# Attention, MoE and FFN in one kernel: V's two heads laid on alternating partitions, both loads on SP's queue

## The chip, the core and the metric

The kernel runs on one core of a Trainium2 chip. The core has a matrix engine (TensorE, PE in the profile, with its weight loads as PEld), three engines for elementwise work (VectorE as DVE, ScalarE as ACT, GpSimd as POOL), a sequencer that only issues (SyncE, SP) and 16 DMA engines that all queues share. The metric is the device time of one execution in microseconds (us); less is better.

## The reference

Three steps follow one another: attention over chunks of 32 queries with a context of 56 keys plus 8 memory keys, a mixture of 8 experts with one expert per token, and a dense FFN. The attention is what the change touches.

```python
# q, k, v: (4, 8, 768, 64) f32; mem_k, mem_v: (4, 8, 8, 64)
for c in range(S // 32):
    l_start, r_end = max(0, 32 * c - 16), min(S, 32 * c + 32 + 8)
    k_full = concat([mem_k, k[:, :, l_start:r_end]], axis=2)
    v_full = concat([mem_v, v[:, :, l_start:r_end]], axis=2)
    scores = (q_c @ k_full.T) / 8
    a = exp(scores - max(scores)); a = a / (sum(a) + 1e-9)
    out_c = a @ v_full
...
x = moe(out.reshape(3072, 512))      # top-1 of 8 experts, w1: 512x1024, w2: 1024x512
return (relu(x @ w_in) ** 2) @ w_out # 512x2048, 2048x512
```

## The kernel before, in words

The host lays q and k out as (batch, pair of heads, 128, 768), two heads of 64 dimensions on 128 partitions, and cuts v into windows: for each batch and head 64 rows (56 context keys and 8 memory keys) of 24 chunks by 64 dimensions, 6 KB per row.

`attention` runs over 32 steps `i`: 4 batches, 4 pairs of heads, 2 halves of 384 queries. One step works on both heads of a pair for 12 chunks. The loop is software-pipelined; in iteration `i` the list `order` calls, in this sequence:

- `stage_b(i)` on PE: scores of 12 chunks (24 matmul passes) into the PSUM tile `sp`. The moving operand is `kw`, the key windows of a pair: head 0 on partitions 0 to 63, head 1 on 64 to 127, each head with columns of its own and zeros in the other's, so that one matmul makes the scores of both heads. `sp` is (query, tile, head, key).
- `stage_d(i-2)` on PE: P times V into `op`, 12 chunks. V's tile `vb` is block-shaped too: head 0's 64 key rows on partitions 0 to 63 in the columns of head 0, head 1's on 64 to 127 in those of head 1, zeros elsewhere.
- `stage_m`, `sum_b(i-1)`, `inv_b(i-1)`, `max_b(i)`, `sub_b(i)`: the logits of the router on PE; row sums, reciprocals, row maxima and the subtraction on DVE.
- `stage_c(i-1)` on PE: the transpose of `e` into `tp`, which ACT copies to `pt`, the stationary operand of `stage_d`. Its partitions are (head, key), the order of `vb`'s rows.
- `exp_b(i)` on ACT, `scale_d(i-2)` on DVE (into `xa`), `stage_t`, `stage_u`.

After the list, `windows(i+2)` lets POOL copy the key windows into `kw` (three buffers), one copy per head and one for the memory keys. When `i` is even the loads of the coming pair go out: `load_v(j)` for `i//2+1` (three buffers `vb`), `load_k` for `i//2+3` (three `kt`), `load_q` for `i//2+2` (three `q`). `load_k` and `load_q` use SP's queue. `load_v` sends head 0 by SP's queue and head 1 by ACT's, 384 KB each. An engine's queue is in order: ACT reaches its V load only after the copies and exponentials ahead of it. ACT's queue also sends the attention's output `x_d` in writes of 768 KB, two at the end of a batch (L376).

`chores` and `early` put other work into the same iterations: clearing `vb` (L413) and the expert embedding's norm in iterations 0 to 4 (`start_en`, a chain of small DVE instructions that `finish_en` waits for), the first part of the routing later. After the attention come the routing, the experts' matmuls and the FFN, all paced by PE.

Of the kernel before, what the change touches and what calls it, by code (L numbers as in the profile page):

```python
# [9 lines left out]
F32 = mybir.dt.float32  # L10
# [4 lines left out]
ALU = mybir.AluOpType  # L15
AX = mybir.AxisListType
# [5 lines left out]
def kernel(  # L22
# [14 lines left out]
    nc = tc.nc  # L37
    P = 128
    B, HP, _, S = q.shape
    H, D, NM = 2 * HP, P // 2, mem_k.shape[3]  # L40
    CH, LEFT, RIGHT = 32, 16, 8
    CTX = LEFT + CH + RIGHT
    HALF = S // 2
    NC = HALF // CH
    HT = HALF // P
# [12 lines left out]
    NEG = -3.0e38  # L58
# [6 lines left out]
    def view(ap, off, dims):  # L65
        return bass.AP(tensor=ap.tensor, offset=ap.offset + off, ap=[list(ap.ap[0])] + dims)
# [12 lines left out]
    ident = const.tile([P, P], F32, name="ident")  # L79
# [49 lines left out]
    def copy(eng, out, in_):  # L129
        if eng == "a":  # L130
            nc.scalar.copy(out=out, in_=in_)
        else:
            (nc.vector if eng == "v" else nc.gpsimd).tensor_copy(out=out, in_=in_)  # L133
# [75 lines left out]
    kw = dict(reuse_waits="tile")  # L209
# [19 lines left out]
    def attention(actx, hooks, space, drain):  # L229
        x_p = actx.enter_context(tc.tile_pool(name="x", bufs=4))  # L230
        wk = actx.enter_context(tc.tile_pool(name="wk", bufs=3))
        per = actx.enter_context(tc.tile_pool(name="per", bufs=1))
        vb_p = actx.enter_context(tc.tile_pool(name="vb", bufs=1))
        qk_ctx = actx.enter_context(ExitStack())
        k_p = qk_ctx.enter_context(tc.tile_pool(name="kw", bufs=1))
        q_p = qk_ctx.enter_context(tc.tile_pool(name="qt", bufs=3))
        ps_a = actx.enter_context(tc.tile_pool(name="ps_a", bufs=2, space=PSUM))
        ps_s, ps_t, ps_o = ps_r
        ps_s2 = actx.enter_context(tc.tile_pool(name="ps_s2", bufs=1, space=PSUM))
        ps_l = actx.enter_context(tc.tile_pool(name="ps_l", bufs=2, space=PSUM))  # L240

        NV, NW, NK_, LAG = 3, 3, 3, 2
        kt = [k_p.tile([P, LEFT + S + RIGHT], F32, name=f"kt{i}") for i in range(NK_)]
        kw = [k_p.tile([P, 2, NC, 64], F32, name=f"kw{i}") for i in range(NW)]
        vb = [vb_p.tile([P, 2, 2 * NC, D], F32, name=f"vb{i}") for i in range(NV)]
        scratch = per.tile([P, TE * P // 2], F32, name="scratch")
        mks = scratch[:, 0:HP * B * NM].rearrange("p (a b m) -> p a b m", a=HP, b=B)
        mkT = per.tile([P, HP, B, 2, NM], F32, name="mkT")
        en = scratch[0:E, B * 2 * D:B * 2 * D + DM]
        enT = per.tile([P, KD, 32], F32, name="enT")  # L250

# [2 lines left out]
        q_t, x_t, st, sums, lp = {}, {}, {}, {}, {}  # L254
# [6 lines left out]
        def load_k(j):  # L261
            b, hp, _ = ks[2 * j]
            nc.sync.dma_start(out=kt[j % NK_][:, LEFT:LEFT + S], in_=k[b, hp])

        def load_v(j):
            b, hp, _ = ks[2 * j]
            for hh in range(2):
                (nc.sync, nc.scalar)[hh].dma_start(out=vb[j % NV][64 * hh:64 * hh + 64, hh], in_=v[b, 2 * hp + hh])

        def windows(i):  # L270

            b, hp, half = ks[i]
            kwt, ktt = kw[i % NW], kt[i // 2 % NK_]
            for hh in range(2):
                src = view(ktt[64 * hh:64 * hh + 64], half * HALF, [[CH, NC], [1, CTX]])
                copy("p" if i > 1 or hh else "a", kwt[64 * hh:64 * hh + 64, hh, :, 0:CTX], src)
            nc.gpsimd.tensor_copy(  # L277
                out=kwt[:, :, :, CTX:64], in_=mkT[:, hp, b].unsqueeze(2).to_broadcast([P, 2, NC, NM])
            )

        def stage_b(i):
            b, hp, half = ks[i]
            qt, kwt = q_t[i // 2], kw[i % NW]
            sp = (ps_s, ps_s2)[i % 2].tile([P, HT, 2, 64], F32, name="sp", tag="s")
            for c in range(NC):
                j, c0 = c % 4, half * HALF + CH * c
                nc.tensor.matmul(  # L287
                    out=sp[32 * j:32 * j + 32, c // 4],
                    lhsT=qt[:, c0:c0 + CH],
                    rhs=kwt[:, :, c, :],  # L290
                    start=True, stop=True,
                    tile_position=(0, 32 * j),
                )

            if half == 0:
                nc.vector.memset(sp[0:32, 0, :, 0:LEFT], NEG)
            else:
                nc.vector.memset(sp[96:128, HT - 1, :, CTX - RIGHT:CTX], NEG)
            st[i] = sp

        def max_b(i):
            mx = wk.tile([P, HT, 2, 1], F32, name="mx", tag="mx")
            nc.vector.tensor_reduce(out=mx, in_=st[i], op=ALU.max, axis=AX.X)
            st[i] = (st[i], mx)

        def sub_b(i):
            sp, mx = st[i]
            e = wk.tile([P, HT, 2, 64], F32, name="e", tag="e")
            nc.vector.tensor_tensor(out=e, in0=sp, in1=mx.to_broadcast([P, HT, 2, 64]), op=ALU.subtract)
            st[i] = e  # L310

        def exp_b(i):
# [2 lines left out]
        def sum_b(i):  # L315
            half = i % 2
            if not half:
                sums[i // 2] = wk.tile([P, 2, HT, 2, 1], F32, name="rs", tag="rs")
            nc.vector.tensor_reduce(out=sums[i // 2][:, half], in_=st[i], op=ALU.add, axis=AX.X)

        def inv_b(i):

# [5 lines left out]
        def stage_c(i):  # L328
            e = st.pop(i)
            tp = ps_t.tile([P, HT, P], F32, name="tp", tag="t")  # L330
            for t in range(HT):
                nc.tensor.transpose(tp[:, t, :], e[:, t].rearrange("p h k -> p (h k)"), ident)
            pt = wk.tile([P, HT, P], F32, name="pt", tag="pt", bufs=2)
            copy("a", pt, tp)
            st[i] = pt
# [71 lines left out]

        def clear_kw(j, eng):
            for hh in range(2):
                eng.memset(kw[j][64 * hh:64 * hh + 64, 1 - hh], 0.0)  # L410

        def clear_v(j, hh, eng):
            eng.memset(vb[j][64 * hh:64 * hh + 64, 1 - hh], 0.0)  # L413

        taub = per.tile([E, 1], F32, name="taub")
        ensq = per.tile([E, 1], F32, name="ensq")
# [2 lines left out]
        def load_en():  # L419
            nc.sync.dma_start(out=en, in_=emb)  # L420
            nc.sync.dma_start(out=taub, in_=tau.to_broadcast([E, 1]))
# [6 lines left out]
        load_q(0)  # L428
        load_en()
        load_k(1)  # L430
        load_v(0)
        nc.vector.memset(mkT, 0.0)
        nc.gpsimd.memset(enT, 0.0)
        for j in range(2):
            clear_kw(j, nc.vector)
        make_identity(nc, ident)
        nc.vector.tensor_copy(out=identr, in_=ident)
        for hh in range(2):
            nc.vector.tensor_copy(out=mkT[64 * hh:64 * hh + 64, :, :, hh, :], in_=mks[64 * hh:64 * hh + 64])
        windows(0)  # L440
        windows(1)
        for hh in range(2):
            clear_v(0, hh, nc.vector)
        clear_kw(2, nc.vector)
        def start_en():
            sq = wk.tile([P, DM], F32, name="sq", tag="sq", bufs=1)
# [9 lines left out]
        def finish_en():  # L456
# [4 lines left out]

        cst = {"scratch": scratch}
        chores = {
            0: [lambda: clear_v(1, 0, nc.gpsimd)],
            1: [start_en, lambda: clear_v(1, 1, nc.gpsimd)],
            2: [lambda: clear_v(2, 0, nc.vector)],
            3: [lambda: clear_v(2, 1, nc.vector)],
            4: [finish_en],
            8: [lambda: cst.update(routing_consts(route, per))],
        }  # L470
# [2 lines left out]
        fill = lambda i: vec.pop(0)() if vec else None  # L473
        order = [
            (stage_b, 0), (stage_d, LAG), (stage_m, LAG + 2), (sum_b, 1), (fill, 0), (inv_b, 1), (max_b, 0), (fill, 0), (sub_b, 0),
            (stage_c, 1), (fill, 0), (exp_b, 0), (scale_d, LAG), (fill, 0), (stage_t, LAG + 1),
            (stage_u, LAG + 3),
        ]
# [12 lines left out]
        for i in range(NK + LAG + 3):  # L491
            if i == NK:
                qk_ctx.close()
                space()
            for f in chores.get(i, []):
                f()
            for f, lag in order:
                if lag <= i < NK + lag:
                    f(i - lag)
                if stage_of(i):  # L500
                    wait[0] = next(early, None) == 1
                drain((i - NK, order.index((f, lag))))
            while vec and i > 2:
                vec.pop(0)()
            if i == starts[0] - 1:
                early = hooks(cst, per, ps_a)
            if i + 2 < NK:
                windows(i + 2)
            if i % 2 == 0:
                for f, n in ((load_v, 1), (load_k, 3), (load_q, 2)):  # L510
                    if i // 2 + n < NK // 2:
                        f(i // 2 + n)
            drain((i - NK, -1))
            for _ in range(min(len(squares), 1 if i < NK else 0)):
                square(*squares.pop(0))
            j = i - LAG
            if 0 <= j < NK and ks[j][1] == HP - 1:
                squares.extend((j, t) for t in range(HT))
# [671 lines left out]
    with tc.manual_schedule():  # L1190
# [65 lines left out]
        def run(ops):  # L1256
            for op in ops.split():
                seq[op[0]](int(op[1:] or 0))
# [8 lines left out]
        with ExitStack() as actx:  # L1267
            c = attention(actx, hooks, space, lambda n: run({(0, -1): 'W0', (1, -1): 'x0 x1 q', (2, -1): 'A0 p q W1 q', (3, -1): 'p q p q', (4, -1): 'N q q q p'}.get(n, "")))
# [168 lines left out]
```

## Time and profile before

| what | value |
|---|---|
| median of 3 runs | 1070.81 us (1069.92 to 1073.3) |
| the profiled execution | 1070.65 us, its span 1068.5 us |
| PE busy over the span | 1005.4 us (94%) |
| DVE, ACT, POOL busy | 528.9, 406.7, 207.4 us |
| attention's steps, first to last scores on PE | 7.91 to 123.3 us |
| mean DMA busy share and rate in 28.2 to 122.4 us | 0.91, 251 GB/s |
| mean DMA busy share and rate in 260 to 340 us | 0.50, 162 GB/s |

The share of busy time is an average over stages with different limits: the attention, the routing, the experts and the FFN have to be read one by one. The DMA share counts the time that packets took on the 16 DMA engines, so it can pass 1 where packets overlap; the rate beside it says what they moved.

### The profile page before, as it was taken

What the parts mean: (1) busy time and instruction counts of PE and PEld (TensorE: products, weight loads), DVE (VectorE), ACT (ScalarE), POOL (GpSimd) and SP (SyncE); (2) the same over time, 40 slices, a digit from 0 to 9 for tenths busy, and PEclk for the clock granted to TensorE, in tenths of its full rate; (3) what the DMA queues carried; (4) which work ended last, traced back from release to release, by engine and by line L of the source; (5) the groups of instructions that cost most, each with busy time, mean ns of one, the idle gap of its engine ahead of it and who ended that gap; (6) DMA issues with size and microseconds to landing.
All of it is one profiled execution on the core that took longest, in us unless ns stands there. A gap on an engine that the chain in (4) does not pass through costs nothing. (4 is left out here: it accounts for less than half of the span.)

```text
span 1068.5 us, 19359 instructions
## 1 busy us (share of the span) xinstructions
PE 1005.4 (94%) x7280; PEld 866.2 (81%) x7280; DVE 528.9 (49%) x1024; ACT 406.7 (38%) x759; POOL 207.4 (19%) x251
## 2 busy tenths in 40 slices
PE   3977788999999999999989999999999999999997
PEld 2766656888888888878778999899998999999896
DVE  7767776575655648958872323222232223323221
ACT  2445452465545546845542222222222222222221
POOL 5545201232323323323220000000000000000000
PEclk9889889999999999999999999999999999999999
DMA  9899820673725447944620101001010100101000
GB/s 235 228 254 277 270 106 30 211 244 123 236 82 184 144 145 254 300 158 139 196 99 9 40 1 40 20 21 40 1 41 2 39 30 11 40 1 40 1 21 20
DMA packets 50006, 115.71 MB, mean 108 GB/s; under 512 B 5345, under 2 KB 5473, under 8 KB 49904
## 3 DMA queue, kind: packets, MB, share of 16 engines
q1 hardware_dynamic: 30192, 65.10, 20.0%
q10 hardware_dynamic: 12896, 27.79, 8.6%
q0 software_dynamic: 6816, 21.50, 5.6%
q8 instruction: 58, 0.95, 0.4%
q14 instruction: 44, 0.36, 0.1%
HBM read 168.90 MB, written 19.92 MB: 177 GB/s over the span
## 5 line engine op out<-in xcount | busy, mean ns | idle before, releaser
L1151 PE MATMUL z<-ft,win_h 128*128 128x256 f32 x768 | 217.3, 283 | 0.5 <-PEq L1380 0.5
L1152 PE MATMUL z<-ft,win_h 128*128 128x256 f32 x768 | 215.6, 281 | 1.9 <-DVE ft L106 1.9
L1153 PE MATMUL z<-ft,win_l 128*128 128x256 f32 x768 | 216.8, 282 | 0.0
L1156 DVE TENSOR_TENSOR r<-r 128x512 f32<-128x512 f32 x96 | 66.5, 693 | 172.3 <-ACT r L1155 172.3
L1152 PEld LDWEIGHTS z<-ft,win_h 128*128 128x128 f32 x768 | 145.9, 190 | 5.7 <-DVE ft L106 2.5
L1151 PEld LDWEIGHTS z<-ft,win_h 128*128 128x128 f32 x768 | 144.2, 188 | 4.1 <-issue 0.9
L106 DVE TENSOR_TENSOR ft<-r,ft 128x512 fp32r<-128x512 f32 x96 | 66.5, 692 | 158.9 <-ACT ft L103 158.9
L1153 PEld LDWEIGHTS z<-ft,win_l 128*128 128x128 f32 x768 | 143.7, 187 | 0.0
L1155 ACT ACTIVATE r<-z 128x512 f32<-128x512 f32 x96 | 57.2, 596 | 180.0 <-PE z L1153 179.2
L103 ACT CAST ft<-r 128x512 fp32r<-128x512 f32 x96 | 59.5, 620 | 168.5 <-PE acc L1175 142.7
L1185 POOL DMA_INDIRECT out_dram<-osb,oid x24 | 27.0, 1123 | 482.3 <-ACT osb L1181 450.5
L133 POOL COPY kw<-kt 64x672 f32<-64x672 f32 x62 | 46.2, 746 | 48.7 <-PE sp L287 43.5
L1108 POOL DMA_INDIRECT y_d<-ysb,sidx x28 | 30.0, 1071 | 127.9 <-ACT ysb L1107 88.4
L344 PE MATMUL op<-vb,pt 128*32 128x128 f32 x768 | 31.3, 297 | 17.6 <-DMA vb<-in_v_dram 8.6
L1060 PE MATMUL yps<-wh2a,hTha 128*128 128x512 f32 x104 | 43.7, 420 | 0.0
L1060 PE MATMUL yps<-wh2b,hThb 128*128 128x512 f32 x104 | 42.6, 410 | 0.0
L1060 PE MATMUL hps<-wh1b,xTh 128*128 128x512 f32 x100 | 41.4, 414 | 0.4 <-ACT ha L1077 0.4
L1062 PE MATMUL yps<-wh2a,hTla 128*128 128x512 f32 x104 | 41.6, 400 | 0.0
L988 POOL DMA_INDIRECT mx<-x_d,gid x28 | 32.1, 1145 | 49.2 <-DVE esf L852 27.7
L344 PEld LDWEIGHTS op<-vb,pt 128*32 128x32 f32 x768 | 23.6, 119 | 22.2 <-issue 11.8
L1061 PE MATMUL yps<-wl2a,hTha 128*128 128x512 f32 x104 | 41.2, 396 | 0.2 <-DVEq L950 0.2
L287 PE MATMUL sp<-kw,q 128*32 128x128 f32 x768 | 31.4, 304 | 10.0 <-POOL kw L277 7.9
(334 smaller groups left out, 2301.2 us busy)
## 6 DMA issues: line engine op xcount, KB each, us to landing
r1a<-in_moe_w_dram SPq DMA_DIRECT2D x52, 512.0 KB
r1b<-in_moe_w_dram SPq DMA_DIRECT2D x52, 512.0 KB
r2a<-in_moe_w_dram SPq DMA_DIRECT2D x50, 512.0 KB
r2b<-in_moe_w_dram SPq DMA_DIRECT2D x50, 512.0 KB
rw<-in_moe_w_in_dram ACTq DMA_DIRECT2D x32, 256.0 KB
rw<-in_moe_w_out_dram ACTq DMA_DIRECT2D x32, 256.0 KB
kt<-in_k_dram SPq DMA_DIRECT2D x16, 384.0 KB
vb<-in_v_dram ACTq DMA_DIRECT2D x16, 384.0 KB
```

The lines of the kernel that those rows point to most:

```text
L103: nc.scalar.copy(out=hi, in_=src)
L106: eng.tensor_tensor(out=lo, in0=src, in1=hi.bitcast(F32), op=ALU.subtract)
L133: (nc.vector if eng == "v" else nc.gpsimd).tensor_copy(out=out, in_=in_)
L344: nc.tensor.matmul(out=op[32 * j:32 * j + 32, c // 4], lhsT=pt[:, c // 4, 32 * j:32 * j + 32], rhs=vt[:, :, c0 + c, :], start=True, stop=True,
L1060: nc.tensor.matmul(out=out_ps, lhsT=ah, rhs=wh, start=first, stop=False)
L1061: nc.tensor.matmul(out=out_ps, lhsT=ah, rhs=wl, start=False, stop=False)
L1062: nc.tensor.matmul(out=out_ps, lhsT=al, rhs=wh, start=False, stop=last)
L1151: nc.tensor.matmul(out=z[:, i, :], lhsT=wh, rhs=yh[:, kk, :], start=(kk == 0), stop=False)
L1152: nc.tensor.matmul(out=z[:, i, :], lhsT=wh, rhs=yl[:, kk, :], start=False, stop=False)
L1153: nc.tensor.matmul(out=z[:, i, :], lhsT=wl, rhs=yh[:, kk, :], start=False, stop=(kk == KD - 1))
L1155: nc.scalar.activation(out=r, in_=z, func=ACTF.Relu)
L1156: nc.vector.tensor_tensor(out=r, in0=r, in1=r, op=ALU.mult)
```

## The change

V's heads alternate on the partitions: head 0's 64 rows go to partitions 0, 2, 4, ..., head 1's to 1, 3, 5, .... P must then have the order (key, head) on its partitions, so the columns of `kw`, `sp` and `e` become (key, head) too: the key windows are written with a step of two elements, the row maximum reads PSUM and the row sum reads SBUF with that step, and the scores' matmul reads one contiguous run of 128 columns where it read two of 64. Both V loads go by SP's queue. A clearing of `vb` now covers all 128 partitions of one head's columns, so it must be over before that buffer's load, where before it touched other partitions than the load did: buffer 0 is cleared by POOL ahead of its first load, buffer 1 by DVE in the setup, buffer 2 by POOL in iterations 0 and 1, and the two clearings by DVE in iterations 2 and 3 are gone.

```diff
-        kw = [k_p.tile([P, 2, NC, 64], F32, name=f"kw{i}") for i in range(NW)]
+        kw = [k_p.tile([P, NC, 64, 2], F32, name=f"kw{i}") for i in range(NW)]
...
-                (nc.sync, nc.scalar)[hh].dma_start(out=vb[j % NV][64 * hh:64 * hh + 64, hh], in_=v[b, 2 * hp + hh])
+                nc.sync.dma_start(out=vb[j % NV][hh:P:2, hh], in_=v[b, 2 * hp + hh])
...
-                copy("p" if i > 1 or hh else "a", kwt[64 * hh:64 * hh + 64, hh, :, 0:CTX], src)
+                copy("p" if i > 1 or hh else "a", kwt[64 * hh:64 * hh + 64, :, 0:CTX, hh], src)
             nc.gpsimd.tensor_copy(
-                out=kwt[:, :, :, CTX:64], in_=mkT[:, hp, b].unsqueeze(2).to_broadcast([P, 2, NC, NM])
+                out=kwt[:, :, CTX:64], in_=mkT[:, hp, b].unsqueeze(1).to_broadcast([P, NC, NM, 2])
             )
...
-            sp = (ps_s, ps_s2)[i % 2].tile([P, HT, 2, 64], F32, name="sp", tag="s")
+            sp = (ps_s, ps_s2)[i % 2].tile([P, HT, 64, 2], F32, name="sp", tag="s")
...
-                    rhs=kwt[:, :, c, :],
+                    rhs=kwt[:, c],
...
-            nc.vector.tensor_reduce(out=mx, in_=st[i], op=ALU.max, axis=AX.X)
+            nc.vector.tensor_reduce(
+                out=mx.rearrange("p t o h -> p t h o"), in_=st[i].rearrange("p t k h -> p t h k"), op=ALU.max, axis=AX.X
+            )
...
-            nc.vector.tensor_tensor(out=e, in0=sp, in1=mx.to_broadcast([P, HT, 2, 64]), op=ALU.subtract)
+            nc.vector.tensor_tensor(out=e, in0=sp, in1=mx.to_broadcast([P, HT, 64, 2]), op=ALU.subtract)
...
-            nc.vector.tensor_reduce(out=sums[i // 2][:, half], in_=st[i], op=ALU.add, axis=AX.X)
+            nc.vector.tensor_reduce(out=sums[i // 2][:, half], in_=st[i].rearrange("p t k h -> p t h k"), op=ALU.add, axis=AX.X)
...
-            eng.memset(vb[j][64 * hh:64 * hh + 64, 1 - hh], 0.0)
+            eng.memset(vb[j][:, hh], 0.0)
...
+        for hh in range(2):
+            clear_v(0, hh, nc.gpsimd)
         load_v(0)
...
         for hh in range(2):
-            clear_v(0, hh, nc.vector)
+            clear_v(1, hh, nc.vector)
...
         chores = {
-            0: [lambda: clear_v(1, 0, nc.gpsimd)],
-            1: [start_en, lambda: clear_v(1, 1, nc.gpsimd)],
-            2: [lambda: clear_v(2, 0, nc.vector)],
-            3: [lambda: clear_v(2, 1, nc.vector)],
+            0: [lambda: clear_v(2, 0, nc.gpsimd)],
+            1: [start_en, lambda: clear_v(2, 1, nc.gpsimd)],
```

ACT's queue at the start of the kernel, before: V's loads of head 1 (`vb_134` to `vb_136` are the three buffers) stand between the copies of `pt` and `xt` and the exponentials `e`.

```order
L268 DMA vb_134<-in_v_dram 64x1536
L131 ACT_TABLE_LOAD
L131 COPY kw_131<-kt_128 64x12x56
L131 COPY kw_132<-kt_128 64x12x56
L313 ACTIVATE e<-e 128x384
L268 DMA vb_135<-in_v_dram 64x1536
L447 ACTIVATE sq,ensq<-scratch 8x512
```

The same place after:

```order
L131 ACT_TABLE_LOAD
L131 COPY kw_131<-kt_128 64x12x56
L131 COPY kw_132<-kt_128 64x12x56
L315 ACTIVATE e<-e 128x384
L451 ACTIVATE sq,ensq<-scratch 8x512
```

ACT issues no V load any more; of the loads and writes of the attention only the writes of `x_d` stay on its queue.

SP's queue at the same place, before (`scratch` receives the memory keys, then the expert embedding):

```order
L427 DMA scratch<-in_mem_k_dram 128x128
L259 DMA q<-in_q_dram 128x768
L263 DMA kt_129<-in_k_dram 128x768
L268 DMA vb_134<-in_v_dram 64x1536
L259 DMA q<-in_q_dram 128x768
L263 DMA kt_130<-in_k_dram 128x768
L268 DMA vb_135<-in_v_dram 64x1536
```

And after:

```order
L429 DMA scratch<-in_mem_k_dram 128x128
L259 DMA q<-in_q_dram 128x768
L263 DMA kt_129<-in_k_dram 128x768
L268 DMA vb_134<-in_v_dram 64x1536 x2
L259 DMA q<-in_q_dram 128x768
L263 DMA kt_130<-in_k_dram 128x768
L268 DMA vb_135<-in_v_dram 64x1536 x2
```

Each V load is now two in a row on SP's queue, and the K and Q loads of the same iteration stand behind both.

DVE in iterations 2 and 3, before: the clearings of the third V buffer stand within the chain of the embedding's norm (`ens`, `ent`).

```order
L122 SCALAR_TENSOR_TENSOR ent<-ent,ena 8x1
L413 MEMSET vb_136 64x1536
L296 MEMSET sp 32x2x16
L319 TENSOR_REDUCE rs<-e 128x6
L124 SCALAR_TENSOR_TENSOR ens<-ens,ent 8x1
```

And after:

```order
L122 SCALAR_TENSOR_TENSOR ent<-ent,ena 8x1
L296 MEMSET sp 32x32
L321 TENSOR_REDUCE rs<-e 128x6
L124 SCALAR_TENSOR_TENSOR ens<-ens,ent 8x1
```

The clearing is gone from DVE here; POOL does it in iterations 0 and 1, where it cleared the second buffer before.

## Rows read from the trace of the kernel before

**Rows 1.** The page's busy time over the whole span: engine, us, share, instructions.

```profile
PE 1005.4 (94%) x7280; PEld 866.2 (81%) x7280; DVE 528.9 (49%) x1024; ACT 406.7 (38%) x759; POOL 207.4 (19%) x251
```

**Rows 2.** Busy time by stretches, in us from the span's start: length, each engine's busy us (and instructions), granted TensorE clock, mean busy share of the 16 DMA engines, GB/s.

```profile
8.00:28.00 20.00, 10.57 (x159) 7.63 (x160) 16.92 (x44) 4.62 (x10) 12.67 (x19) 0.98 1.03 241
...
28.20:122.40 94.20, 77.68 (x1648) 62.40 (x1647) 65.81 (x200) 46.71 (x119) 46.15 (x77) 0.91 0.91 251
...
122.00:140.00 18.00, 12.48 (x170) 8.97 (x169) 14.35 (x39) 8.65 (x19) 3.86 (x4) 0.71 0.92 327
...
180.00:260.00 80.00, 79.45 (x408) 65.28 (x407) 51.36 (x87) 43.69 (x74) 20.23 (x20) 1.00 0.56 182
260.00:340.00 80.00, 80.00 (x394) 66.04 (x393) 42.26 (x78) 40.01 (x76) 24.11 (x26) 1.00 0.50 162
```

**Rows 3.** The timeline, PE alone: start us, length us, and the 24 matmul passes of one `stage_b`. These are iteration 4, iterations 7 to 9, and iteration 31, the last.

```profile
28.21 1.51 PE L287 MATMUL sp<-kw,q 128*32 128x128 f32 x24
...
38.33 0.86 PE L287 MATMUL sp<-kw,q 128*32 128x128 f32 x24
...
41.28 0.86 PE L287 MATMUL sp<-kw,q 128*32 128x128 f32 x24
...
43.74 0.86 PE L287 MATMUL sp<-kw,q 128*32 128x128 f32 x24
...
122.40 0.86 PE L287 MATMUL sp<-kw,q 128*32 128x128 f32 x24
```

**Rows 4.** The timeline again: the issues of V's seventh pair on SP's and ACT's queue, of an `x_d` write on ACT's queue between them, and the first matmuls of `stage_d` that read that pair (idle us before it, and what ended that); then the issues of V's ninth pair.

```profile
46.02 0.47 SPq L268 DMA_DIRECT2D vb<-in_v_dram  x1
...
46.81 0.41 ACTq L376 DMA_DIRECT2D x_d<-xa  x1
...
50.78 0.49 ACTq L268 DMA_DIRECT2D vb<-in_v_dram  x1
...
57.47 0.47 SPq L268 DMA_DIRECT2D vb<-in_v_dram  x1
...
65.42 0.87 PE L344 MATMUL op<-vb,pt 128*32 128x128 f32 x12 [6.20 <-DMA vb<-in_v_dram]
...
68.67 0.47 ACTq L268 DMA_DIRECT2D vb<-in_v_dram  x1
```

**Rows 5.** The page's DMA issues: queue, count, KB each.

```profile
kt<-in_k_dram SPq DMA_DIRECT2D x16, 384.0 KB
vb<-in_v_dram ACTq DMA_DIRECT2D x16, 384.0 KB
q<-in_q_dram SPq DMA_DIRECT2D x16, 384.0 KB
vb<-in_v_dram SPq DMA_DIRECT2D x16, 384.0 KB
...
x_d<-xa ACTq DMA_DIRECT2D x6, 768.0 KB
```

**Rows 6.** Who waited for whom, 28 to 125 us for PE's rows, 28 to 122 us for SP's queue: us in total, times, longest.

```profile
PE op L344 <- DMA vb<-in_v_dram: 8.6, 2, 6.2
...
PEld op L344 <- issue: 11.8, 4, 6.4
...
SPq L268 <- PE op L344: 34.6, 8, 10.5
...
SPq L268 <- DMA x_d<-xa: 6.8, 2, 3.7
```

**Rows 7.** Groups of instructions by line and shape, 0 to 260 us: busy us, mean ns of one, idle before. The two reductions of every iteration, then reductions of a small tile out of PSUM with a step of 8 elements (`e_cs`) and out of SBUF without a step (`km`), reductions out of SBUF with (`oh`) and without (`lt`) a step, the write of `lt` with a step and of `oh` without, and POOL's copy of the key windows.

```profile
L319 DVE TENSOR_REDUCE rs<-e 128x6 f32<-128x384 f32 x32 | 17.1, 533 | 5.7 <-ACT e L313 3.6 <-ACT xt L131 2.0
L303 DVE TENSOR_REDUCE mx<-sp 128x6 f32<-128x384 f32 x32 | 16.7, 522 | 0.0
...
L570 DVE TENSOR_REDUCE km<-ge 128x6 f32<-128x48 f32 x4 | 0.8, 204 | 0.1
...
L589 DVE TENSOR_TENSOR lt<-km,rev 128x144 f32<-128x144 f32 x1 | 0.4, 396 | 0.0
...
L591 DVE TENSOR_REDUCE sums<-oh 128x8 f32<-128x144 bf16 x1 | 0.3, 336 | 0.0
...
L587 DVE TENSOR_TENSOR oh<-rev,km 128x144 bf16<-128x144 f32 x1 | 0.3, 296 | 0.0
L593 DVE TENSOR_REDUCE sums<-lt 128x8 f32<-128x144 f32 x1 | 0.3, 292 | 0.0
...
L627 DVE TENSOR_REDUCE e_cs<-cp 128x8 f32<-128x48 f32 x1 | 0.2, 197 | 0.0
...
L133 POOL COPY kw<-kt 64x672 f32<-64x672 f32 x62 | 46.2, 746 | 48.7 <-PE sp L287 43.5 <-DMA kt<-in_k_dram 3.3
```

**Rows 8.** The timeline of the first 28 us: ACT's first V load, DVE's copy of the memory keys, the first row maximum, the two clearings of the third buffer, and the matmuls that end the embedding's norm.

```profile
0.77 0.56 ACTq L268 DMA_DIRECT2D vb<-in_v_dram  x1
...
6.93 0.46 DVE L439 COPY mkT<-scratch 64x128 f32<-64x128 f32 x2 [1.34 <-DMA scratch<-in_mem_k_dram]
...
17.43 1.34 DVE L413 MEMSET vb<- 64x1536 f32 x1 [0.27 <-issue]
...
22.45 1.34 DVE L413 MEMSET vb<- 64x1536 f32 x1 [0.38 <-issue]
...
27.69 0.59 PE L459 MATMUL ep<-ident,scratch 8*128 8x8 f32 x4 [4.14 <-DVE scratch L453]
```

More of the change, by code (lines that the diff above doesn't have):

```diff
@@ L247, in attention @@
         mks = scratch[:, 0:HP * B * NM].rearrange("p (a b m) -> p a b m", a=HP, b=B)
-        mkT = per.tile([P, HP, B, 2, NM], F32, name="mkT")
+        mkT = per.tile([P, HP, B, NM, 2], F32, name="mkT")
         en = scratch[0:E, B * 2 * D:B * 2 * D + DM]
@@ L295, in stage_b @@
             if half == 0:
-                nc.vector.memset(sp[0:32, 0, :, 0:LEFT], NEG)
+                nc.vector.memset(sp[0:32, 0, 0:LEFT], NEG)
             else:
-                nc.vector.memset(sp[96:128, HT - 1, :, CTX - RIGHT:CTX], NEG)
+                nc.vector.memset(sp[96:128, HT - 1, CTX - RIGHT:CTX], NEG)
             st[i] = sp
         def max_b(i):
-            mx = wk.tile([P, HT, 2, 1], F32, name="mx", tag="mx")
-            nc.vector.tensor_reduce(out=mx, in_=st[i], op=ALU.max, axis=AX.X)
+            mx = wk.tile([P, HT, 1, 2], F32, name="mx", tag="mx")
+            nc.vector.tensor_reduce(
+                out=mx.rearrange("p t o h -> p t h o"), in_=st[i].rearrange("p t k h -> p t h k"), op=ALU.max, axis=AX.X
+            )
             st[i] = (st[i], mx)
@@ L307, in sub_b @@
             sp, mx = st[i]
-            e = wk.tile([P, HT, 2, 64], F32, name="e", tag="e")
-            nc.vector.tensor_tensor(out=e, in0=sp, in1=mx.to_broadcast([P, HT, 2, 64]), op=ALU.subtract)
+            e = wk.tile([P, HT, 64, 2], F32, name="e", tag="e")
+            nc.vector.tensor_tensor(out=e, in0=sp, in1=mx.to_broadcast([P, HT, 64, 2]), op=ALU.subtract)
             st[i] = e
@@ L331, in stage_c @@
             for t in range(HT):
-                nc.tensor.transpose(tp[:, t, :], e[:, t].rearrange("p h k -> p (h k)"), ident)
+                nc.tensor.transpose(tp[:, t, :], e[:, t].rearrange("p k h -> p (k h)"), ident)
             pt = wk.tile([P, HT, P], F32, name="pt", tag="pt", bufs=2)
@@ L409, in clear_kw @@
             for hh in range(2):
-                eng.memset(kw[j][64 * hh:64 * hh + 64, 1 - hh], 0.0)
+                eng.memset(kw[j][64 * hh:64 * hh + 64, :, :, 1 - hh], 0.0)
         def clear_v(j, hh, eng):
-            eng.memset(vb[j][64 * hh:64 * hh + 64, 1 - hh], 0.0)
+            eng.memset(vb[j][:, hh], 0.0)
         taub = per.tile([E, 1], F32, name="taub")
@@ L438, in attention @@
         for hh in range(2):
-            nc.vector.tensor_copy(out=mkT[64 * hh:64 * hh + 64, :, :, hh, :], in_=mks[64 * hh:64 * hh + 64])
+            nc.vector.tensor_copy(out=mkT[64 * hh:64 * hh + 64, :, :, :, hh], in_=mks[64 * hh:64 * hh + 64])
         windows(0)
```

## The prediction

> **What bounds the kernel now.** Over the span PE is busy 94% [rows 1], but that mixes stages. By stretches [rows 2], from 180 us on PE is busy 79.45 of 80 and then 80 of 80 us at full clock with the DMA engines half idle: the experts and the FFN are PE's, and nothing of this change is in them. From 28.2 to 122.4 us, most of the attention, PE is busy 77.68 and DVE 65.81 of 94.2 us, while the DMA engines are at 0.91. So in the attention I look at the DMAs first.
>
> Three readings bear that out. The undisturbed pace of the loop: iterations 7, 8 and 9 start at 38.33, 41.28 and 43.74 [rows 3], a pair of iterations in 5.41 us. Iterations 4 to 31 start at 28.21 and 122.40 [rows 3]: 27 iterations in 94.19 us, 6.98 us per pair. At the undisturbed pace they would take 13.5 x 5.41 = 73.0 us. 21 us are lost on the way.
>
> Where they are lost: iteration 12's `stage_d` starts at 65.42 after 6.20 us of idle that a V load ended [rows 4]. PE waited 8.6 us in two such waits, and its weight loads ahead of the same stage 11.8 us in four waits put down to "issue" [rows 6]; the longest, 6.4 us, is the same place, so these are in good part the same waits. The load that ended the wait is ACT's: SP issued its half of that V pair at 46.02, ACT at 50.78, after a write of `x_d` on the same queue at 46.81 [rows 4]. ACT's half of V was used 14.6 us after its issue. Two pairs later SP issued at 57.47 and ACT at 68.67: ACT is in order, and reached its load only when PE ran again.
>
> Why a load takes so long: the stretch moved 251 GB/s at a share of 0.91, so 276 GB/s at full share. The stretch of 122 to 140 us moved 327 at 0.92, 355 at full share, and 180 to 260 us 182 at 0.56, 325 [rows 2]. The attention's transfers fill the engines and get a fifth less out of them.
>
> **The change part by part.** V's rate. Per pair of iterations the loads are 2 x 384 KB of V, 384 of K and 384 of Q [rows 5], and a batch of four pairs writes 2 x 768 KB, 384 KB per pair: V is 40% of the bytes. The stretch moved 251 x 94.2 us = 23.6 MB, which at 276 GB/s is 85.7 us of full engines. If the other 60%, 14.2 MB, run at 340 GB/s (between 325 and 355), they take 41.7 us; V's 9.45 MB take the other 44.0, 215 GB/s. V's loads are the only ones with 64 partitions, and the layout is what the change alters. The two ends: V stays at 215, and the floor of the stretch stays 85.7 us; or V reaches 340, takes 27.8, and the floor is 69.5. No row shows a load of 64 alternating partitions. I take half of the rise, 277 GB/s: 34.1 us, a floor of 75.8.
>
> [...]
>
> V's queue. The second half of each V pair is issued some 0.5 us after the first instead of 4.8 to 11.2 us later [rows 4], and not behind `x_d` writes. Half of V in time doesn't help `stage_d`; now both are. ACT saves 16 issues of 0.47 us [rows 4, 5], which I count as nothing, because PE and DVE set the undisturbed pace. What it costs: SP's queue carries 16 more issues, 0.5 us per 5.41 us pair, and K and Q stand behind both halves. K and Q are loaded several iterations ahead, and SP spent 34.6 us waiting for PE to free V's buffers [rows 6], so it has room.
>
> Steps of two elements. `max_b` reads PSUM with a step. The nearest row is `e_cs`, 48 elements out of PSUM with a step of 8: 197 ns, against 204 for 48 out of SBUF without a step [rows 7]. So nothing (B is the case that the row misleads, since it is a short one). `sum_b` reads SBUF with a step: 336 ns with one against 292 without, for 144 elements, +15% [rows 7]; on 533 ns that is 0.08 us, over 27 iterations 0 to 2.2 us. I take 1. POOL writes `kw` with a step: no such row on POOL. On DVE 396 against 296 ns, a third more [rows 7]; two copies of 746 ns would become 2.0 us per iteration, below the pace of 2.7, and POOL now waits 43.5 us for PE [rows 7]. Nothing, unless a copy doubles. The matmuls and the transposes read as many columns as before: nothing.
>
> Start. ACT's V load at 0.77 us goes out ahead of the memory keys, for which DVE waits 1.34 us [rows 8]; now V comes behind them. Two clearings of 1.34 us with 0.27 and 0.38 us of idle leave DVE at 17.43 and 22.45, within the chain for which PE waits 4.14 us at 27.69 [rows 8], just before iteration 4: 3.3 us. POOL's two clearings ahead of the first V load fall into a time in which it waits 3.3 us for K's first load [rows 7]: nothing. SP's first V load waits for them, but if one takes POOL what it takes DVE, 1.34 us [rows 8], that is under 3 us, and five issues stand ahead of it anyway. Against that, the DMA engines are full between 8 and 28 us [rows 2], so part of the 4.6 us may turn into waiting for loads; I take 3.5.
>
> Sum. Main stretch: the pace alone gives 73.0 us plus some 4 for the routing's small DVE work in it (an estimate: a dozen instructions of about 0.2 us for each of the later batches, and as much again for its constants), 77. The DMA floor is 75.8. Two limits so close don't overlap fully; I keep idle DMA time at nearly the present 9%, which gives 75.8 / 0.92 = 82, plus 1 for the reductions: 83 against 94.2, 11.2 us less. With 3.5 from the start it is 14.7. What follows (the routing, which the iterations pace, then PE) shifts as a whole, since its weights are asked for by the same chain. The profiled execution took 1070.65 us with a span of 1068.5, 0.16 below the median 1070.81. 1070.65 - 14.7 = 1056.
>
> **Rivals.** *A: the rate stays.* The two halves of V are still two transfers, and one behind the other they use the engines as before. Then the floor is 85.7 us, at a share of 0.97 88.4: 5.8 us less, and nothing at the start, where the engines are full: 1065 (1062 to 1068). For it: no row shows V faster. Against: weights loaded at 355. [...]
>
> *B: the stepped reductions double.* Then each iteration costs DVE 533 + 522 ns more [rows 7]: 77 + 28.5 = 105.5 us instead of 94.2, +11.3, and about 4.2 in the first four iterations against the 3.5 saved, +1 for the last: 1084. It decides from 0.3 us per reduction on: (94.2 - 77) / 27 = 0.64 us per iteration eat the gain. Against it: the row of `e_cs`. Only `max_b` doubled would be 0.52 x 27 = 14.1 us, which takes the whole gain and ends at 1070. [...]
>
> *C: SP's queue becomes the limit.* A V load on SP that waits for a buffer or behind an `x_d` write (6.8 us now, [rows 6]) holds K and Q, and `stage_b` waits where `stage_d` did. If the second half doubles that and PE's weight loads keep their 11.8 us [rows 6], the gain of 14.7 shrinks to about 14.7 - 6.8 - 5.9 = 2: 1068.6, no change.
>
> **How the numbers follow.** Forecast 0.62 (1047 to 1062), A 0.20, C 0.11, B 0.07. The low end is the pace alone with all of the start: 73.0 us, so 21.2 + 4.6 = 25.8 less would be 1045, which needs DMAs that never wait; 1047 leaves little below. The high end takes in A and stops at 1067; C and B lie beyond. About 0.3%, 3.2 us, is what a measurement of this kernel can tell from no change. Faster by more: the forecast and nearly all of A, 0.81. Same: C and the rest of A, 0.11. Slower: B and a C that is worse than priced, 0.08.
>
> **What would show it.** Rate: the attention's stretch moves 300 GB/s or more at full share. Queue: no idle of `stage_d` before V; the two SP issues of a pair lie next to each other. Pace: the scores of iteration 31 start some 14 us earlier, at 108; of iteration 4 at about 24.7. The reductions stay at 520 to 610 ns, POOL's copies under 1.0 us. From there to the end everything is as long as before. Wrong would be: V's rate unchanged (A), reductions of 0.85 us and more (B), PE idle before `stage_b` for K or Q (C).

## The result, and the profile after

| | before | after |
|---|---|---|
| median, us | 1071.17 (4 runs, 1069.92 to 1073.3) | 1051.41 (4 runs, 1050.72 to 1052.38) |
| profiled execution, us (its span) | 1070.65 (1068.5) | 1051.24 (1049.1) |

The ratio is 0.9821, with a 95% interval of 0.9804 to 0.9838: the changed kernel is 1.8% faster. The forecast was 1056 us in a range of 1047 to 1067; 1051.4 lies in it, 4.6 us below the forecast.

The page's busy time over the whole span of the changed kernel, to set beside [rows 1]:

```profile
PE 1000.8 (95%) x7280; PEld 863.0 (82%) x7280; DVE 526.8 (50%) x1022; ACT 406.9 (39%) x759; POOL 213.9 (20%) x253
```

The engines do the same work within 7 us each. So the gain is idle time that has gone, and the stretches show where. Busy time by stretches, columns as in [rows 2]: the start, iterations 4 to 31, the routing, and two pieces of the part that PE paces.

```profile
8.00:28.00 20.00, 13.87 (x255) 10.47 (x247) 17.18 (x53) 5.79 (x13) 14.93 (x22) 1.00 0.77 287
...
22.90:101.96 79.06, 72.37 (x1649) 57.81 (x1648) 66.79 (x200) 47.12 (x119) 49.76 (x77) 1.00 0.85 297
...
104.00:122.00 18.00, 13.83 (x151) 9.64 (x152) 12.67 (x32) 9.56 (x20) 3.85 (x4) 0.67 0.92 333
...
160.00:240.00 80.00, 79.44 (x408) 65.25 (x407) 51.10 (x87) 43.34 (x73) 20.16 (x20) 1.00 0.55 182
240.00:320.00 80.00, 80.00 (x394) 66.04 (x394) 42.33 (x77) 40.01 (x76) 23.74 (x26) 1.00 0.50 161
```

The second row carries the result. Before, the same 1648 matmul passes took 94.20 us at 251 GB/s and a share of 0.91, 276 GB/s at full share. Now they take 79.06 us at 297 GB/s and 0.85: 349 GB/s at full share, about what the stretches without V loads reached before (355 and 325). (At full share means the rate divided by the DMA share.) Full engines alone do not make this quotient low: the third row has a share of 0.92 and 362 GB/s at full share. Nor did the transfers get fewer or larger: the page counts 50006 packets before and after.

TensorE's granted clock was 0.91 of full speed on average and is 1.00 now. The scores of iteration 4, just behind a wait of 4.14 us [rows 8], took 1.51 us before [rows 3], at a granted clock of 0.50 from 28.2 to 29.8 us; now they take 0.86, at 1.00. That goes with PE's busy time of 72.37 instead of 77.68 us. The scores' matmul, which reads one run of 128 columns now, is not the gain: at a granted clock of 1.00 its 24 passes took 0.86 us before too [rows 3]. PE's stretches read as before; the routing is looked at below.

The timeline, PE alone, as [rows 3]: the scores of iteration 4 and of iteration 31.

```profile
22.90 0.86 PE L287 MATMUL sp<-kw,q 128*32 128x128 f32 x24
...
101.96 0.86 PE L287 MATMUL sp<-kw,q 128*32 128x128 f32 x24
```

They split the gain. To iteration 4: 28.21 - 22.90 = 5.3 us. From there to iteration 31: 94.2 - 79.1 = 15.1 us. From there to the end of the span: 947.1 against 1068.5 - 122.40 = 946.1, 1.0 us given back. Together 19.4, the difference of the spans.

Who waited for whom from 22.9 to 101.96 us, as [rows 6]: us in total, times, longest.

```profile
PEld op L346 <- issue: 2.3, 2, 1.3
...
POOL kw L133 <- PE sp L287: 20.7, 23, 3.4
...
SPq L268 <- PE op L346: 21.8, 7, 5.7
SPq L268 <- DMA x_d<-xa: 13.9, 2, 7.3
...
SPq L259 <- DMA x_d<-xa: 6.4, 1, 6.4
```

No row of PE waiting for `vb` is left, where there were 8.6 us, and the weight loads of `stage_d` wait 2.3 us for their issue where they waited 11.8 [rows 6]. SP's queue waits 13.9 us for `x_d` writes at V's loads, where it waited 6.8 [rows 6], and 6.4 at Q's (L259). Q's row before, from the same view as [rows 6]:

```profile
SPq L259 <- DMA x_d<-xa: 5.8, 3, 3.3
```

Together 20.3 us instead of 12.6, nearly as long as for PE. The semaphores in the trace tell what these waits are. Each transfer carries a semaphore that counts up, 16 times, as it lands. The transfers that SP and ACT issue in this stretch share eight of them, and all 52 that follow another on their semaphore go out after that one has landed. V's load of 48.79 us carries the semaphore of the `x_d` write that ACT issued at 39.41, and goes out when that write has landed, at 48.72. So the wait is one that the program asks for. What it costs is asked below.

Groups of instructions by line and shape, 0 to 260 us, as [rows 7]: busy us, mean ns of one, idle before.

```profile
L321 DVE TENSOR_REDUCE rs<-e 128x6 f32<-128x384 f32 x32 | 17.2, 538 | 0.9 <-ACT e L315 0.7
L303 DVE TENSOR_REDUCE mx<-sp 128x6 f32<-128x384 f32 x32 | 16.8, 524 | 0.0
...
L133 POOL COPY kw<-kt 64x672 f32<-64x672 f32 x62 | 50.6, 815 | 24.5 <-PE sp L287 20.7 <-DMA kt<-in_k_dram 1.8
```

The stepped reductions cost what the others did: 538 against 533 ns, 524 against 522. POOL's copies with a step on the output take 815 against 746 ns, 9% more, beside 24.5 us of idle.

The timeline of the start, as [rows 8]: POOL's clearings of the first V buffer, V's first two loads, DVE's copy of the memory keys, the first scores, and the matmuls that end the embedding's norm.

```profile
0.75 2.69 POOL L415 MEMSET vb<- 128x1536 f32 x2 [0.29 <-POOLq L1421]
...
3.29 1.20 SPq L268 DMA_DIRECT2D vb<-in_v_dram  x2
...
4.99 0.45 DVE L443 COPY mkT<-scratch 64x128 f32<-64x128 f32 x2
...
6.50 2.79 PE L287 MATMUL sp<-kw,q 128*32 128x128 f32 x48 [6.50 <-DMA q<-in_q_dram]
...
22.56 0.41 PE L463 MATMUL ep<-ident,scratch 8*128 8x8 f32 x4 [2.36 <-DVE scratch L457]
```

The memory keys are copied at 4.99 instead of 6.93, and the norm ends 5.1 us earlier.

### The profile page after: what moved, and what is told of

Its sections match the earlier page's. It is cut to its first block, busy times and chain, and to the rows that moved or that the text cites. A ratio compares the mean times of both kernels' runs of the same rounds, so it can differ in the third digit from the quotient of the medians.

```text
span 1049.1 us, 19355 instructions
## 1 busy us (share of the span) xinstructions
PE 1000.8 (95%) x7280; PEld 863.0 (82%) x7280; DVE 526.8 (50%) x1022; ACT 406.9 (39%) x759; POOL 213.9 (20%) x253
## 2 busy tenths in 40 slices
DMA packets 50006, 115.71 MB, mean 110 GB/s; under 512 B 5345, under 2 KB 5473, under 8 KB 49904
## 3 DMA queue, kind: packets, MB, share of 16 engines
q1 hardware_dynamic: 31472, 71.40, 20.4%
## 5 line engine op out<-in xcount | busy, mean ns | idle before, releaser
L133 POOL COPY kw<-kt 64x672 f32<-64x672 f32 x62 | 50.6, 815 | 24.5 <-PE sp L287 20.7
L1062 PE MATMUL hps<-wh1b,xTh 128*128 128x512 f32 x100 | 41.4, 414 | 0.4 <-ACT ha L1079 0.4
L1064 PE MATMUL yps<-wh2b,hTlb 128*128 128x512 f32 x104 | 40.7, 391 | 0.0
L1063 PE MATMUL yps<-wl2b,hThb 128*128 128x512 f32 x104 | 40.6, 391 | 0.0
L205 POOL TENSOR_TENSOR win_l<-wf,win_h 128x256 fp32r<-128x256 f32 x32 | 25.5, 797 | 73.5 <-ACT win_h L204 68.1
```

Of the source, the lines that this page charges most:

```text
L1062: nc.tensor.matmul(out=out_ps, lhsT=ah, rhs=wh, start=first, stop=False)
L1063: nc.tensor.matmul(out=out_ps, lhsT=ah, rhs=wl, start=False, stop=False)
L1064: nc.tensor.matmul(out=out_ps, lhsT=al, rhs=wh, start=False, stop=last)
```

## The experiments

Each ratio is against the kernel before, run on the same chip, with its 95% interval. A stretch is always from the scores of iteration 4 to those of iteration 31: 94.2 us before, 79.1 after. The theory that came out of the first reading, called R below: the 64 neighbouring partitions of a V load hold back the transfer, alternating partitions don't, and everything else in the change is small. Its rival Q: the gain is the second half of V leaving ACT's queue.

### The layout alone, and the queue alone

The first is the changed kernel with head 1's V on ACT's queue again: the layout, with the clearings that it needs. The second is the kernel before with both halves on SP's queue.

```diff
-                nc.sync.dma_start(out=vb[j % NV][hh:P:2, hh], in_=v[b, 2 * hp + hh])
+                (nc.sync, nc.scalar)[hh].dma_start(out=vb[j % NV][hh:P:2, hh], in_=v[b, 2 * hp + hh])
```

> The changed kernel with head 1's V load back on ACT's queue: alternating partitions without the move to SP. Theory R (the layout raises V's rate, and that is most of the gain): iterations 4 to 31 take about 82 us (94.2 before, 79.1 after), the rate at full DMA share stays near 340 GB/s, 1055 us in all, a little lost at the start because V stands ahead of the memory keys again. Theory Q (V's second half comes in time because SP issues it, and that is most of the gain): about 90 us for these iterations and 1063 us, with PE idle before stage_d for V.

```diff
-                (nc.sync, nc.scalar)[hh].dma_start(out=vb[j % NV][64 * hh:64 * hh + 64, hh], in_=v[b, 2 * hp + hh])
+                nc.sync.dma_start(out=vb[j % NV][64 * hh:64 * hh + 64, hh], in_=v[b, 2 * hp + hh])
```

> The kernel before with both V loads on SP's queue and nothing else changed: 64 neighbouring partitions per load. Theory R: the rate at full share stays near 276 GB/s, iterations 4 to 31 take about 90 us, 1066 us in all. Theory Q: about 83 us, 1058 us, although the rate stays.

Layout alone: 1051.81 us, ratio 0.9836 (0.9817 to 0.9856). Queue alone: 1065.82 us, 0.9952 (0.9931 to 0.9973). The stretch of the layout alone, measured, as all stretches here, in the one profiled execution:

```profile
22.97:102.24 79.27, 71.57 (x1649) 57.62 (x1647) 66.53 (x200) 46.85 (x119) 49.60 (x77) 1.00 0.85 297
```

What PE still waits for V in it:

```profile
PE op L346 <- DMA vb<-in_v_dram: 1.6, 1, 1.6
```

The stretch of the queue alone, and SP's longest waits in it:

```profile
26.16:118.09 91.93, 77.32 (x1648) 61.28 (x1647) 66.41 (x200) 46.98 (x119) 46.15 (x77) 0.94 0.98 266
```

```profile
SPq L268 <- DMA x_d<-xa: 26.8, 4, 10.9
```

The layout alone gives the changed kernel's stretch, rate and time; with it, it does not matter who issues V. Q is out. In the old layout the queue is worth 0.5%: the engines go from 0.91 to 0.98 busy, at 271 GB/s per full share, so two halves next to each other fill the idle time, and the rate stays.

### The clearings alone

The kernel before with the clearings in the changed kernel's places.

```diff
+        for hh in range(2):
+            clear_v(0, hh, nc.gpsimd)
         load_v(0)
...
-            clear_v(0, hh, nc.vector)
+            clear_v(1, hh, nc.vector)
...
-            0: [lambda: clear_v(1, 0, nc.gpsimd)],
-            1: [start_en, lambda: clear_v(1, 1, nc.gpsimd)],
-            2: [lambda: clear_v(2, 0, nc.vector)],
-            3: [lambda: clear_v(2, 1, nc.vector)],
+            0: [lambda: clear_v(2, 0, nc.gpsimd)],
+            1: [start_en, lambda: clear_v(2, 1, nc.gpsimd)],
```

> The kernel before with the new places of V's clearings alone (POOL clears buffer 0 ahead of the loads and buffer 2 in iterations 0 and 1, DVE buffer 1 in the setup). If DVE's chain sets the start: iteration 4 starts 3.3 us earlier, at 24.9 us, and the whole gains some 3 us, 1068. If the full DMA engines set it, or if the loads eat it later: iteration 31 starts as before at 122.4 and the time is unchanged, 1071.

1064.98 us, 0.9956 (0.9939 to 0.9973). Its stretch, and what PE still waits for in it:

```profile
24.18:117.87 93.69, 77.61 (x1650) 61.88 (x1648) 66.90 (x206) 47.47 (x120) 46.17 (x77) 0.93 0.96 266
```

```profile
PE op L344 <- DMA vb<-in_v_dram: 12.0, 3, 4.7
```

Iteration 4 starts at 24.18 where it started at 28.21: the new places of the clearings bring 4.0 us of the start, 0.5 of it ahead of the first scores (7.40 instead of 7.91). The stretch keeps its pace: 277 GB/s at full share, and PE waits for V. The time is 3 us below the expected 1068; of the profiled span 2.1 us more are gained behind iteration 31 (944.0 instead of 946.1 us), of which more below. This kernel and the one with the layout alone differ in the layout and what belongs to it alone: 1064.98 against 1051.81 us, a stretch of 93.7 against 79.3.

### Half of V

The changed kernel without head 1's V loads. It leaves out half of V, so half of the attention's output is missing and its time as a whole is not read, only the stretch.

```diff
-            for hh in range(2):
+            for hh in range(1):
                 nc.sync.dma_start(out=vb[j % NV][hh:P:2, hh], in_=v[b, 2 * hp + hh])
```

> The changed kernel without head 1's V loads: head 1's columns of the attention come from a cleared buffer, so the routing and all behind it see other data, and only the stretch of the attention's iterations is read. If loads still limit the changed kernel's main stretch, iterations 4 to 31 fall from 79.1 to about 74 us, the undisturbed pace. If PE and DVE limit it: 78 us or more, while the DMA share falls from 0.85 to about 0.65.

```profile
23.24:103.68 80.44, 73.18 (x1650) 59.12 (x1648) 67.31 (x200) 47.12 (x119) 49.70 (x77) 0.98 0.66 227
```

The DMA share falls from 0.85 to 0.66 and the stretch does not get shorter (80.4 against 79.1, one execution each). In the changed kernel the loads no longer set the pace of the stretch.

### K and Q in halves

If R holds, it must work on other tiles too. In the changed kernel K's and Q's loads are cut in two, once as neighbouring halves, once, as a control with the same number of transfers, as alternating halves.

```diff
-            nc.sync.dma_start(out=q_t[j], in_=q[b, hp])
+            for z in range(2):
+                nc.sync.dma_start(out=q_t[j][64 * z:64 * z + 64], in_=q[b, hp, 64 * z:64 * z + 64])
...
-            nc.sync.dma_start(out=kt[j % NK_][:, LEFT:LEFT + S], in_=k[b, hp])
+            for z in range(2):
+                nc.sync.dma_start(out=kt[j % NK_][64 * z:64 * z + 64, LEFT:LEFT + S], in_=k[b, hp, 64 * z:64 * z + 64])
```

> The changed kernel, with every K and Q load cut into two loads of 64 neighbouring partitions (0 to 63, 64 to 127), all on SP's queue; the same bytes to the same places. Theory R (64 neighbouring partitions take the rate down, wherever the bytes go): K and Q are as many bytes as V, so the rate at full share falls from 347 to about 276 GB/s as in the kernel before, iterations 4 to 31 take 88 us or more (79.1 in the changed kernel), 1061 us or more. If V's gain had another cause than its partitions: the same as the control with alternating halves.

```diff
+            for z in range(2):
+                nc.sync.dma_start(out=q_t[j][z:P:2], in_=q[b, hp, z:P:2])
...
+            for z in range(2):
+                nc.sync.dma_start(out=kt[j % NK_][z:P:2, LEFT:LEFT + S], in_=k[b, hp, z:P:2])
```

> The control to the run with neighbouring halves: K and Q loads cut in two as well, but into the even and the odd partitions. Theory R: the rate at full share stays near 340 GB/s, iterations 4 to 31 take 79 to 81 us, 1051 to 1053 us. If the number and size of the loads on SP's queue are what costs: as slow as the run with neighbouring halves.

Neighbouring halves: 1069.65 us, 0.999 (0.9971 to 1.0009), the whole gain gone. Its stretch and waits:

```profile
23.74:120.78 97.04, 78.95 (x1650) 63.73 (x1648) 67.46 (x200) 46.83 (x119) 49.64 (x77) 0.91 0.89 252
```

```profile
SPq L260 <- DMA x_d<-xa: 19.3, 3, 6.8
...
PE sp L289 <- DMA q<-in_q_dram: 7.7, 3, 4.0
```

Alternating halves: 1062.08 us, 0.9929 (0.9908 to 0.9949). Its stretch and waits:

```profile
23.28:112.19 88.91, 75.89 (x1650) 61.00 (x1648) 66.56 (x200) 46.95 (x119) 49.62 (x77) 0.94 0.75 265
```

```profile
SPq L260 <- DMA x_d<-xa: 20.4, 3, 7.0
...
PEld sp L289 <- issue: 10.4, 22, 3.3
...
PE sp L289 <- DMA q<-in_q_dram: 3.6, 2, 2.0
```

The rates say it plainly: at full share 252 / 0.89 = 283 GB/s with neighbouring halves of K and Q, 265 / 0.75 = 353 with alternating ones, for the same bytes in the same number of transfers; and 8.1 us of stretch between the two. SP's waits for `x_d` are alike in both (19.3 and 20.4 us), so they are not the difference. K and Q are together as many bytes as V, and the slow case has the rate that the kernel before had with V in neighbouring halves (276).

But the control missed its time: the stretch was to be 79 to 81 us and took 88.9, with the DMA engines a quarter idle. The rows show SP at its loads of Q (L260), waiting 20.4 us for writes of `x_d`, and PE's scores waiting for Q. That is the rival C of the prediction. The next run tests it.

### The alternating halves, with `x_d` written by POOL

```diff
-                (nc.gpsimd if b == B - 1 else nc.scalar).dma_start(out=x_d[T0 * P:(T0 + HT) * P, :].rearrange("(t p) d -> p t d", p=P), in_=xa)
+                nc.gpsimd.dma_start(out=x_d[T0 * P:(T0 + HT) * P, :].rearrange("(t p) d -> p t d", p=P), in_=xa)
```

> The run with K and Q in alternating halves, with all writes of x_d issued by POOL. There SP's queue waited 20.4 us for writes of x_d to land, with K and Q behind. Theory W (those waits are what the 10 us of that run are): SP no longer waits for x_d, iterations 4 to 31 fall from 88.9 to about 80 us, 1053 us. If the number and size of the loads are what costs: 88 us and 1061 us as before.

1053.11 us, 0.9832 (0.9805 to 0.9858), 9.0 us less than with `x_d` on ACT's queue. The stretch, and SP's longest wait in it:

```profile
23.72:106.09 82.37, 74.82 (x1648) 59.68 (x1648) 68.31 (x200) 46.87 (x119) 53.92 (x83) 0.97 0.81 286
```

```profile
SPq L270 <- PE op L348: 17.4, 9, 6.9
```

SP waits for PE now, not for `x_d`, since the writes that POOL issues carry semaphores of their own (in the changed kernel's trace its two carry two that no transfer of SP or ACT has), and the control runs within 2 us of the changed kernel. So most of its miss, 6.5 of 9.8 us of stretch, was SP held by the `x_d` writes. The other 3.3 us, in a profiled execution of 1055.11 us where the four runs lie between 1050.73 and 1055.3, may be a price of the halves; that stays open.

### Less in the start, and `x_d` on POOL without the halves

The changed kernel, with V's second buffer cleared by two copies on ACT out of a cleared column, instead of by DVE in the setup; and the same with `x_d` written by POOL.

```diff
+        nc.gpsimd.memset(enT, 0.0)
...
+            nc.scalar.copy(out=vb[1][:, hh], in_=enT[:, 0:1, 31:32].to_broadcast([P, 2 * NC, D]))
...
-        nc.gpsimd.memset(enT, 0.0)
...
-        for hh in range(2):
-            clear_v(1, hh, nc.vector)
```

> The changed kernel with V's second buffer cleared by ACT (two copies of a cleared column while it waits for the first K load) instead of by DVE in the setup. If DVE's chain sets the start: its two clearings of 1.34 us with the idle ahead of them are gone, ACT's first window copies come some 0.6 us later, iteration 4 starts at about 20.3 us instead of 22.9, and the whole takes about 1049 us. If the loads or PE set the start: 22.9 and 1051.4.

> The run with the second V buffer cleared by ACT, with all writes of x_d issued by POOL. SP waited 20.7 us for x_d there, but PE did not wait for loads. If SP's waits cost nothing where DVE and PE set the pace: the same 1050 us within 2 us. If the writes on POOL hold back the window copies: slower, 1052 or more. If SP's waits still cost: 1047.

ACT's clearing: 1050.12 us, 0.9815 (0.9798 to 0.9831). With `x_d` on POOL too: 1050.80 us, 0.9822 (0.9804 to 0.9839). Their stretches, first the one, then the other:

```profile
21.14:100.80 79.66, 71.86 (x1650) 57.67 (x1648) 67.68 (x200) 47.21 (x119) 49.72 (x77) 1.00 0.85 294
```

```profile
21.11:101.96 80.85, 73.42 (x1649) 59.18 (x1647) 67.61 (x200) 46.87 (x119) 54.14 (x83) 0.98 0.82 289
```

Iteration 4 starts 1.8 us earlier than in the changed kernel, less than the 2.6 expected, and of that 1.2 are left at iteration 31. The interval overlaps the changed kernel's, so that this version is faster is not shown. Moving `x_d` away brings nothing here, though SP waited 20.7 us for it in the version with ACT's clearing, as long as in the changed kernel (20.3). So these waits cost nothing that the move gives back. The move has a price of its own, 4.4 us more of POOL's busy time (54.14 against 49.72), and that a small gain hides behind it is not excluded.

### Queue and clearings together, in the old layout

Both edits shown above, put into the kernel before.

> The kernel before with all of the change except the partitions: both V loads on SP's queue and the clearings at their new places. Theory R: the start gains some 4 to 5 us, iterations 4 to 31 stay at 90 us or more with the rate near 276 GB/s at full share, 1061 to 1065 us. Were the queue and the clearings together enough: 83 us or less, 1055.

1069.11 us, 0.9988 (0.9976 to 1.0): 4 us more than the clearings alone, 3 more than the queue alone, and above the 1061 to 1065 that R led to expect. Its stretch and waits:

```profile
23.29:120.53 97.24, 76.37 (x1650) 61.07 (x1648) 65.29 (x200) 46.84 (x119) 46.11 (x77) 0.96 0.96 254
```

```profile
SPq L268 <- DMA x_d<-xa: 17.6, 2, 10.5
...
SPq L259 <- DMA x_d<-xa: 8.6, 1, 8.6
...
PE sp L287 <- DMA q<-in_q_dram: 5.8, 5, 2.5
```

The start gains 4.9 us and the stretch, at 265 GB/s per full share, loses 3. Everything in the change but the layout is worth 1.5 us when put together (0 to 2.6 by the interval). SP waits 26.2 us for `x_d` and PE 5.8 for Q, as in the control above; but the queue alone shows SP's wait at 26.8 us and is faster. The load that is held differs: with the queue alone only V's, here also one of Q's, 8.6 us long, and PE waits 5.8 us for Q where it waited 1.4. That this is why the two edits don't add is not shown.

## Why the prediction was right, point by point

**What bounds the kernel.** Right for the kernel before: three runs that keep V's layout keep the slow rate (271, 277 and 265 GB/s at full share) and a stretch of 92 us or more, and the one with the layout and its clearings has 349 and 79.3, of which the clearings alone bring the stretch 0.5 us. TensorE's clock is not what made the stretch long: queue and clearings together have a mean clock of 0.96 and the longest stretch of the three.

**V's rate.** The mechanism was right and its size was off. I took half of the rise, 277 GB/s for V. If the other 60% of the bytes run at 340 as I assumed, the 23.5 MB of the stretch (297 x 79.06 us) at 349 leave V 9.4 MB in 67.3 - 41.4 = 25.9 us, 363 GB/s: the whole rise came. The floor is then 67 us and not 75.8, below the 77 that I had for the engines' pace. "I keep idle DMA time at nearly the present 9%" failed with it: the share fell to 0.85 because nothing waits for loads any more, as half of V shows. The stretch took 79.1, of which I can place 77 by the prediction's own term (its 4 us for the routing's small DVE work is an estimate that no run tested); it was forecast at 83. That 4 us, 1 of it the reductions below, is most of what the forecast missed. So the time fell into the range although the limit that set the forecast of the stretch, the DMA engines, was the wrong one.

Loads cut into neighbouring halves give 276 and 283 GB/s at full share for the mix, alternating ones 349 and 353. V's own rate is worked out, not measured, and why neighbouring partitions are slower no trace here shows.

**V's queue.** The mechanism was half right. V's halves are issued next to each other (3.29 us, 1.20 us for both), and PE no longer waits for V. But the second follows nearly from the layout alone: with half of V on ACT's queue PE waits for it once, 1.6 us. I had not given the queue a term of its own in the stretch, and with the new layout it deserves none (1051.81 against 1051.41 us).

**Steps of two elements.** `max_b` nothing, as said. `sum_b` 5 ns more in 27 iterations, 0.1 us, where I took 1: the two rows that I took it from differ in the element type as well, bf16 against f32 [rows 7]. POOL's copies +9%, within "nothing unless a copy doubles". Rival B, with its half for PSUM alone, is out: VectorE's read of PSUM with the step took 524 ns against 522 without.

**Start.** 5.3 us came where I took 3.5 of 4.6. The two terms were right in kind and a little small: the clearings alone bring 4.0, for which I had 3.3, and the queue alone about 2 (iteration 4 at 26.16), for which I had 1.3. The allowance for full DMA engines was wrong: they are at 0.77 between 8 and 28 us now, not 1.03. That V comes behind the memory keys was right, and the queue does it by itself; what I had not seen is that the layout does it too. With V on ACT's queue its first load waits for POOL's clearing of its buffer (0.75 to 3.44 us), the keys are copied at 4.99 us as well, and the first scores start at 6.50 us. The keys' copy in the kernel with the queue alone:

```profile
4.99 0.45 DVE L439 COPY mkT<-scratch 64x128 f32<-64x128 f32 x2
```

ACT's first V load in the one with the layout alone, at 0.77 us before:

```profile
3.47 0.56 ACTq L268 DMA_DIRECT2D vb<-in_v_dram  x1
```

**Afterwards.** "As long as before" was 1.0 us off. From the scores of iteration 31 to the end, the version with ACT's clearing took 943.5 us in its profiled execution (a span of 1044.3, the fastest of its five), the changed kernel 947.1 and the kernel before 946.1, so that part moves by more than this between kernels that do the same there. TensorE's granted clock differs too: in the three stretches of 20 us from iteration 31 on it was 0.68, 0.98 and 0.91 before and 0.71, 0.95 and 0.83 in the changed kernel; over the whole execution it was 0.982 and 0.988, and 0.995 in the version with ACT's clearing. That the clock is the cause is not shown.

**Rivals.** A is out by the rate. C exists: it costs the control with the alternating halves about 9 us, and moving `x_d` removes that. In the changed kernel SP waits as long for `x_d` (20.3 against 20.4 us), at no cost that the move of `x_d` gave back. That K and Q had twice as many issues behind the wait in the control is a likely reason, but only argued.

**The sum.** Forecast 11.2 + 3.5 + 0 = 14.7; measured 15.1 + 5.3 - 1.0 = 19.4. Most of the error is caution in two terms, both of them about DMA engines that I expected to stay full; 1 us is the reductions' term, and the micro-second afterwards goes the other way.

## What to carry to other kernels

When a stretch is at a DMA share of 0.9, divide its rate by the share and set that beside other stretches of the same kernel: if it is low (276 against 325 and 355 GB/s here), the transfers themselves may be slow, and their shape on the partitions is worth a look before queues and order, as it was here. Two tiles of 64 partitions that are used as one of 128 can be interleaved if the operand on the other side can take the same order, and the steps that this put into VectorE's reductions cost 2 to 5 ns each here. Once the rate was freed, the next limit here was the engines' pace (without half of V the stretch still took 80.4 us), so price the gain up to there and no further, and don't carry the old idle share over (0.09 before, 0.15 after). When a queue stands for another engine's transfer, see whether the two carry the same semaphore: here SP stood for up to 10.9 us at a load for a write of `x_d` that ACT had issued, and in the two runs with the writes issued by POOL no wait of SP for `x_d` is left. That gained nothing in one kernel and 9 us in another; how much SP has queued behind the wait seems to decide, which is not shown.

## What was not expected of the hardware

- Cutting 128-partition loads into two neighbouring halves took the mixed rate from 349 to 283 GB/s and lost the whole gain; cut into alternating halves, the rate stayed at 353.
- A step of two f32 elements on what VectorE reads cost 2 to 5 ns on some 520 to 540, out of PSUM and out of SBUF; on what POOL writes, 69 ns on 746.
